# Orders by place, 64-row output products and TensorE's own waits in a fused attention and dense kernel

## The chip, the core and the metric

The kernel runs on one core of a Trainium2 chip. The metric is the device time of one execution in microseconds. A profiled execution comes with a trace of every instruction; TensorE does the matrix products (PE in the rows, PEld for its weight loads), VectorE is DVE, ScalarE is ACT, GpSimd is POOL, and SyncE is SP, which issues most DMAs.

## The reference

All inputs are float32; x is 2048 x 512, there are 32 heads of 16 columns, and the dense part is 1376 wide.

```python
xn = _layernorm(x)
qkv = (xn @ wqkv) -> q, k, v per head
p = softmax(q @ k.T * 16 ** -0.5)
s = (p @ v, heads side by side) @ wo
g = silu(gelu(xn @ w1 + b1) @ w2 + b2)
out = x + s * g
```

## The kernel before, in words

Products that must be exact are made of rounded halves: an operand is split into a high part (rounded) and a low part (the rest), and a product is three matmuls, high by high, high by low and low by high. The order of each engine's instructions is written out by hand: what stands earlier in the code stands earlier in that engine's queue.

**The dense part (first 476 us).** After the layer norm, the q, k and v projections and the two dense layers are made as pairs of 64-row matmuls: `run` walks two lists of operations, and `mm` (L590) issues one of them on the upper row tile (partitions 0 to 63, a = 0) and one on the lower (64 to 127, a = 1), so that two matmuls go side by side. An accumulator is written first by one row tile, later by the other. When `mm` changes the row tile of an accumulator whose last product isn't known to be over, it makes the matmul wait for a token: `mark` puts a copy of one element on ScalarE (`junk`, L604; twice on VectorE, L602) that waits for the latest product, and the matmul waits for that copy. `mark_early` does this from within the product before. Between the pairs, `fill` puts score tiles of the first units (below).

**The attention part.** The work is 32 units `u`: four heads by 512 queries. A unit has 16 steps of 128 keys, so step `n` has unit `n // 16` and place `n % 16`. A step's order is a string, `ORDER[3]` = T S X T T S T Y V:

- T (`t_one`, L739): scores of 128 keys by 512 queries of one head, on row tile 1, 1, 0, 0 in turn, with the rows' maxima subtracted by two extra rows; ScalarE makes their exponential (L741) into the tile that pv reads one step later. T's go to four PSUM banks.
- S (`s_whole`, L183, L189): scores the other way round, 128 queries by 512 keys, for a unit that comes later, only for the maximum that VectorE takes of them; the first S of a step is on row tile 0, the second on row tile 1.
- X and Y: one such tile of 512 columns in halves, X 256 columns on row tile 0, Y 256 columns on row tile 1 into the same bank. Y waits for X by a no-operation of TensorE that waits for TensorE's own semaphore. VectorE's maximum comes after Y.
- V (`pv_step`, L804): the exponentials of the step before times v, in four column tiles of 32, float32. After the last place of a unit VectorE copies the accumulator out (L811).

S, X and Y use three PSUM banks in turn (`s_ring`): an S takes the oldest bank and puts it at the end of the ring at once, an X takes the oldest bank and its Y puts it back. Score tiles run ahead of T, so from step 492 on there are none, and a step is T T T T V.

**The output product.** `at(n, f, ..., pos)` hangs a piece of work behind T number `pos` of step `n`. In steps 492 to 511 the first ten of sixteen token tiles of 128 rows are multiplied by `wo`. For tile `t`, with n = 492 + 2t: `load_gx` at n - 4 brings the dense result and x; `w_token` at n - 2 rounds the attention output (ScalarE L876, GpSimd L877); `w_mul` (`mm3`, L80) makes six 128-row matmuls at n and six at n + 1, into a bank of the ring; `gate` at n makes the gate (ScalarE L865, VectorE L866); `w_out` at n + 1 multiplies (VectorE L905), adds x (GpSimd L910) and stores. The other six tiles follow after the last step.

Of the kernel before, what the change touches and what calls it, by code (L numbers as in the profile page):

```python
# [8 lines left out]
F32 = mybir.dt.float32  # L9
F32R = mybir.dt.float32r  # L10
AF = mybir.ActivationFunctionType
# [5 lines left out]
P = 128  # L17
# [4 lines left out]
KT = D // P  # L22
NT = S // P
CH = 512
NCH = S // CH
# [10 lines left out]
DONE = 492  # L36
FILL0 = 30
HB = 4
W2B = 2
ORDER = {0: "TTTTV", 3: "TSXTTSTYV"}  # L40
HC = CH // 2
PAIRED = 28
KB = 3
# [5 lines left out]
def fused(ctx: ExitStack, tc: tile.TileContext, x, wqk, wv, wo, w1, b1, w2, b2, out):  # L49
    nc = tc.nc  # L50
# [17 lines left out]
    ident_r = keep.tile([P, P], F32R, name="ident_r")  # L68
# [17 lines left out]
    SYNC = mybir.DependencyInfo(mybir.DependencyClass.Sync, mybir.DependencyReason.DATA)  # L86
# [5 lines left out]
    def s_tile(held=False):  # L92
        pool = s_ring.pop(0)
        if not held:
            s_ring.append(pool)
        return pool.tile([P, CH], F32, name="ps"), pool
# [58 lines left out]
    done = {u: 0 for u in range(NU)}  # L155
# [30 lines left out]
    def s_max(ps, job, heads, parts):  # L186
        u, p = job[0], job[2]
        qi, ki = at_of(job)
        nc.vector.tensor_reduce(MX[u][:, 2 * p:2 * p + 2, qi, ki][:, heads, parts], ps.rearrange("p (n c) -> p n c", c=HC), axis=AX.X, op=OP.max)  # L189
        done[u] += 1  # L190
# [18 lines left out]
    def s_op(op):  # L209
# [6 lines left out]
        elif op == "X":  # L216
            if not cut:
                cut[:] = [jobs.pop(0), 0]
            ps, pool = s_tile(True)
            x = s_mm(ps, cut[0], 0, 0, cut[1] * HC, HC)  # L220
            cut[2:] = [ps, pool, x]
            run_off()
        else:
            job, n, ps, pool, x = cut
            hold = nc.tensor.nop().ins
            tc.add_manual_dep(hold, x.name, SYNC, reason="row tile done")
            s_mm(ps, job, 1, HC, n * HC, HC)
            s_max(ps, job, slice(0, 2), n)
# [33 lines left out]
    prog = {}  # L262
# [42 lines left out]
    for i in range(nu):  # L305
        pairs.append(ms[2 * i:2 * i + 2])
        if (i + 1) * len(qs) // nu > i * len(qs) // nu:
            g, c = qs[i * len(qs) // nu]
            pairs.append([("q", g, c), ("q", g, c + 1)])
    parts = [(c, f, h) for c in range(NCH) for f in range(FT) for h in range(2)]  # L310
    is_m = [pair[0][0] == "m" for pair in pairs]
    plan, nd = [("first", g, i) for g in range(VQ - 1) for i in (0, 2)], 0
    for j in range(len(pairs)):
        for h in range(2):
# [223 lines left out]
    keep_r = ctx.enter_context(tc.tile_pool(name="keep_r", bufs=1, side="right"))  # L538
# [19 lines left out]
    writer = {}  # L558
    s_when, put, row = [], [0], [0, 0]
# [22 lines left out]

    def mm(a, key, ps, lhs, rhs, first, last):
        r = slice(64 * a, 64 * a + 64)
        token = None
        if not first and writer[key][0] != a and writer[key][1] > prog["seen"]:
            if not tokens or tokens[-1][0] < writer[key][1]:
                mark()
            prog["seen"], token = next(x for x in tokens if x[0] >= writer[key][1])
        i = nc.tensor.matmul(ps, lhs[r], rhs[r], start=first, stop=last).ins  # L590
        if token is not None:
            tc.add_manual_dep(i, token, SYNC, reason="other row tile")
        prog["pe"] += 1
        row[a] += 1
        latest[0] = (prog["pe"], i.name)
        writer[key] = (a, prog["pe"])

    tokens, latest = [], [None]

    def mark(dve=False):  # L600
        if dve:
            i = nc.vector.tensor_copy(junk[:, 1:], ident_r[:1, :1].bitcast(F32)).ins  # L602
        else:
            i = nc.scalar.activation(junk[:, :1], ident_r[:1, :1].bitcast(F32), AF.Copy).ins  # L604
        tc.add_manual_dep(i, latest[0][1], SYNC, reason="row tile done")
        tokens.append((latest[0][0], i.name))

    def mark_early(n):
        if prog["seen"] < n:
            mark()  # L610

    junk = keep_r.tile([1, 2], F32, name="junk")

    def run(ops, hooks={}):
        for n, two in enumerate(zip(*ops)):
            prog["n"] += 1
            for a in range(2):
                fill(a)
                mm(a, *two[a])
            for h in hooks.get(n, []):  # L620
                h()
# [23 lines left out]
    def down(c, f, part):  # L645
        i = c * FT + f
        if f == 0 and part == 0:
            PA[c] = [ps_v.tile([P, D], F32, name="pv")] + [ps_t.tile([P, D], F32, name="pst") for t in range(3)]
        h, w = HS[c, f], W2[c, f]
        side = (part + i) % 2  # L650
        ops = [[], []]
        for a in range(2):
            for t in ((0, 1), (2, 3))[(a + side) % 2]:
                ts = slice(t * P, (t + 1) * P)
                for n, (x, y) in enumerate(((0, 0), (0, 1), (1, 0))):
                    ops[a].append(((c, t), PA[c][t], h[x][:, ts], w[y],
                                   f == 0 and part == 0 and n == 0, f == FT - 1 and part == 1 and n == 2))
        n = prog["pe"]
        if (c, f, part) == parts[-2]:
            run(ops, {2: [lambda: mark(True)], 5: [lambda: mark(True)]})  # L660
        else:
            run(ops, {3: [lambda: mark_early(n)]})
        if part == 0:
            w2_split(i + 1)
            w2_load(i + 3)
            return
        del HS[c, f], W2[c, f]
        if f == FT - 1:
            for t in (0, 2, 1, 3):
                gt = wk.tile([P, D], F32, name="gt", bufs=4)  # L670
                if c == NCH - 1:
                    nc.vector.tensor_add(gt, PA[c][t], b2_sb)  # L672
                else:
                    nc.scalar.activation(gt, PA[c][t], AF.Copy)
                rs = slice(c * CH + t * P, c * CH + (t + 1) * P)
                if c < NCH - 1:
                    chores.append((gt, rs))
                else:
                    nc.gpsimd.dma_start(g_d[rs, :], gt)
# [22 lines left out]
    def quad(n, at):  # L702
        us = first[n]
        for u, b in zip(us, BANKS[n]) if at == 0 else ():
            pool, name = {"x": (ps_x, "ps"), "m": (ps_m, "ps"), "v": (ps_v, "pv"), "t": (ps_t, "pst")}[b]
            PH[u] = pool.tile([P, CH], F32, name=name)
        for i in range(at, at + 2):
            hooks = {6: [mark]} if i in (1, 2) else {}
            if n == VQ - 2 and i in (0, 2):
                hooks[3] = [lambda: w1_split(0) if i == 0 else w1_load(1)]  # L710
            run((terms(us[i], 0, i < 2), terms(us[(i + 2) % 4], 1, i < 2)), hooks)
            if i >= 2:
                for u in (us[i - 2], us[i]):
                    v_out(u[1] * NCH + u[2], PH.pop(u))
# [62 lines left out]
    wb = ctx.enter_context(tc.tile_pool(name="work_b", bufs=2))  # L777
    ot = [slot(6 + c, (P, KT, CH)) if c < 2 else kp.tile([P, KT, CH], F32, name=f"ot{c}") for c in range(NCH)]
# [3 lines left out]
    wo_h = kp.tile([P, KT, D], F32R, name="wo_h")  # L782
    wo_l = kp.tile([P, KT, D], F32R, name="wo_l")
# [14 lines left out]
    def pv_step(u, k):  # L798
# [8 lines left out]
        if k == NT - 1:  # L807
# [36 lines left out]
    GX, OTS, PW, homes = {}, {}, {}, {}  # L844
# [47 lines left out]
    def w_mul(t, ks, parts=(0, 1)):  # L892
# [4 lines left out]
        for i, cs in enumerate(cols(t)):  # L897
            if i in parts:
                for k in ks:
                    mm3(PW[t][i][:, :cs.stop - cs.start], OTS[t, k], (wo_h[:, k, cs], wo_l[:, k, cs]),  # L900
                        k == 0, k == KT - 1)

    def w_gate(t, i=0):
        gx, cs = GX[t], cols(t)[i]
        nc.vector.scalar_tensor_tensor(gx[:, 0, cs], PW[t][i][:, :cs.stop - cs.start], 0.5, gx[:, 0, cs],  # L905
                                       op0=OP.mult, op1=OP.mult)
# [12 lines left out]
    def at(n, f, *a, pos=3):  # L919
        todo.setdefault((n, pos), []).append((f, a))  # L920

    KS = tuple(range(KT))
    L = 16 * NU

    def due(n):
        return min(4 * L, 4 * LEAD + max(0, 3 * n - 1))

    for u in range(NU):
        g, c = divmod(u, NCH)
# [15 lines left out]
    T3 = range(NT - NCH, NT)  # L945
    late = range(NW, NT)
    for t in range(NW):
        n = DONE + 2 * t
        at(n - 4, load_gx, t)
        at(n - 2, w_token, t)  # L950
        at(n, w_mul, t, KS[:2])
        at(n, gate, t)
        at(n + 1, w_mul, t, KS[2:])
        at(n + 1, w_out, t, nc.gpsimd)
    for i, t in enumerate(late):
        n = L - 2 * len(late) - 1 + 2 * i
        at(n - 4, load_gx, t)
# [8 lines left out]
    for n in range(L + 1):  # L966
        ua, ka = divmod(n, 16)
        want = due(n) - due(n - 1)
        i = 0
        for op in ORDER[want] if n > 1 else ("TTTTV", "TTSTSVT")[n]:  # L970
            if op in "SXY":
                s_op(op)
            elif op == "V":
                if n:
                    pv_step(*divmod(n - 1, 16))
                for _ in range(4):
                    tick()
# [61 lines left out]
```

## Time and profile before

| | |
|---|---|
| median of three runs | 1581.37 us (1580.71 to 1581.43) |
| the profiled execution | 1580.84 us |
| its span in the trace | 1579.0 us |
| TensorE, weight loads | 1572.2, 949.2 us busy |
| VectorE, ScalarE, GpSimd | 1396.2, 1247.6, 373.6 us busy |
| granted TensorE clock | full (1.0) throughout |

A row of a timeline has the start in the span, the time that it took, the engine, the line, the operation, what it writes and reads, rows*columns and the shape, and a count where several follow one another; in brackets stands the idle time before it and what ended it. A row of the waits has who waited for whom, the sum in us, the number of times and the longest. Starts are what the argument goes by, since matmuls overlap and their ends are modelled. PSUM tiles `ps` and `pst` are score banks, `pv` is the accumulator of V.

### The profile page before, as it was taken

How to read it: one execution, taken by the hardware profiler on the slowest of the kernel's cores; microseconds unless marked ns; L12 is line 12 of the kernel's file. 1: busy time of each engine (PE TensorE's matmuls, PEld its weight loads, DVE VectorE, ACT ScalarE, POOL GpSimd, SP SyncE). 2: the span in 40 equal slices, each digit the busy share in tenths (PEclk: the TensorE clock that was granted, in tenths of full speed). 3: DMA queues.
4: the chain of work that ended last, by engine and by line, in shares of the span. 5: the costliest groups of instructions: out<-in, count | busy, mean ns of one | idle time of the engine just before them, and what ended most of it. 6: DMA issues, size and time to landing. Idle time of an engine off the chain costs nothing.

```text
span 1579.0 us, 31736 instructions
## 1 busy us (share of the span) xinstructions
PE 1572.2 (100%) x12144; PEld 949.2 (60%) x12144; DVE 1396.2 (88%) x2292; ACT 1247.6 (79%) x2489; POOL 373.6 (24%) x394
## 2 busy tenths in 40 slices
PE   9999999999999999999999999999999999999998
PEld 8899899999994444444444444444444444444445
DVE  7599898989988999999999999999999999999734
ACT  4333443434339999999999999999999999999984
POOL 4145575766641001001000100100100000000143
PEclk9999999999999999999999999999999999999999
DMA  6626343454322114111511511421150111110252
GB/s 207 151 59 154 116 138 99 147 150 122 123 84 76 43 33 68 29 36 42 82 30 29 69 38 34 56 45 29 30 76 24 33 29 36 36 30 22 60 194 101
DMA packets 74647, 116.86 MB, mean 74 GB/s; under 512 B 23012, under 2 KB 24292, under 8 KB 73320
## 3 DMA queue, kind: packets, MB, share of 16 engines
q1 hardware_dynamic: 70748, 101.89, 24.1%
q0 software_dynamic: 3264, 12.35, 4.7%
q8 instruction: 96, 1.57, 0.5%
q10 hardware_dynamic: 484, 0.60, 0.1%
q14 instruction: 55, 0.45, 0.1%
HBM read 84.35 MB, written 25.97 MB: 70 GB/s over the span
## 4 chain that ended last, share of the span: by engine, by line
PE 98%; DVE 1%; DMA 0%; issue 0%; ACT 0%; DVEq 0%
PE pv L804 33%; PE pst L739 21%; PE ps L590 13%; PE ps L183 10%; PE pst L590 7%; PE ps L739 7%; PE ps L80 3%; PE pv L590 2%; PE ps L458 1%; PE pst L80 1%; DVE st L417 0%; PE pst L440 0%; DMA xt<-in_x 0%; PE pst L458 0%; DVE slot L75 0%; DVE xn L431 0%
## 5 line engine op out<-in xcount | busy, mean ns | idle before, releaser
L189 DVE TENSOR_REDUCE mx<-ps 128x2 f32<-128x512 f32 x2048 | 1298.3, 685 | 118.6 <-PE ps L183 33.0
L741 ACT ACTIVATE slot<-pst 128x512 f32<-128x512 f32 x1533 | 825.9, 603 | 19.9 <-PE pst L739 10.5
L804 PE MATMUL pv<-slot,vsb 128*32 128x512 f32 x4096 | 545.3, 605 | 0.0
L183 PE MATMUL ps<-kt,slot 48*128 48x512 f32 x1364 | 376.4, 366 | 0.0
L739 PE MATMUL pst<-qt,kt 50*128 50x512 f32 x1149 | 372.3, 431 | 0.6 <-DVE gt L672 0.4
L739 PEld LDWEIGHTS pst<-qt,kt 50*128 50x128 f32 x1149 | 188.6, 184 | 288.3 <-ACT slot L741 261.8
L741 ACT ACTIVATE slot<-ps 128x512 f32<-128x512 f32 x515 | 311.2, 605 | 2.7 <-PE ps L183 1.8
L183 PEld LDWEIGHTS ps<-kt,slot 48*128 48x128 f32 x1364 | 224.7, 184 | 8.2 <-DVE mx L189 5.9
L590 PE MATMUL ps<-slot,w1h 64*128 64x512 f32 x1088 | 218.0, 393 | 0.0
L183 PE MATMUL ps<-kt,qz 48*128 48x512 f32 x512 | 212.8, 416 | 0.0
L183 PE MATMUL ps<-slot,slot 48*128 48x512 f32 x598 | 165.5, 366 | 0.0
L739 PE MATMUL ps<-qt,kt 50*128 50x512 f32 x387 | 159.7, 415 | 0.0
L590 PEld LDWEIGHTS ps<-slot,w1h 64*128 64x128 f32 x1088 | 151.2, 185 | 8.2 <-ACT junk L604 2.4
L590 PE MATMUL ps<-slot,w1l 64*128 64x512 f32 x544 | 141.8, 393 | 0.0
L804 PEld LDWEIGHTS pv<-slot,vsb 128*32 128x32 f32 x4096 | 80.6, 108 | 100.0 <-issue 91.8
L377 POOL TENSOR_TENSOR hl<-hg,hh 128x512 fp32r<-128x512 f32 x76 | 96.7, 1295 | 129.6 <-ACT hh L376 97.5
L250 POOL CAST nmh<-nm 128x16 fp32r<-128x16 f32 x32 | 6.3, 196 | 480.4 <-DVE nm L247 458.0
L604 ACT ACTIVATE junk<-ident_r 1x1 f32<-1x1 f32 x92 | 18.0, 196 | 119.3 <-PE pst L590 116.1
L739 PE MATMUL pst<-qt,slot 50*128 50x512 f32 x384 | 111.2, 414 | 0.0
L183 PEld LDWEIGHTS ps<-kt,qz 48*128 48x128 f32 x512 | 93.7, 183 | 15.6
L183 PEld LDWEIGHTS ps<-slot,slot 48*128 48x128 f32 x598 | 98.3, 184 | 3.1 <-DVE mx L189 2.1
L739 PEld LDWEIGHTS ps<-qt,kt 50*128 50x128 f32 x387 | 71.1, 184 | 42.1 <-ACT slot L741 36.4
(159 smaller groups left out, 1707.2 us busy)
## 6 DMA issues: line engine op xcount, KB each, us to landing
raw<-in_w SPq DMA_DIRECT2D x88, 256.0 KB
qk_h<-hh SPq DMA_DIRECT2D x32, 256.0 KB
qk_l<-hl SPq DMA_DIRECT2D x32, 256.0 KB
qt<-qk_h SPq DMA_DIRECT2D x128, 64.0 KB
slot<-qk_h SPq DMA_DIRECT2D x92, 64.0 KB
g_d<-gt POOLq DMA_DIRECT2D x16, 256.0 KB, 3.8
qt<-qk_l SPq DMA_DIRECT2D x64, 64.0 KB
dn<-den_d SPq DMA_DIRECT2D x32, 128.0 KB
```

The source lines that it names most:

```text
L80: nc.tensor.matmul(ps, lhs[a], rhs[b], start=first and n == 0, stop=last and n == 2)
L183: return nc.tensor.matmul(ps[:, c0:c0 + w], QS[u][r, p, qi * P:(qi + 1) * P], kts[u // NCH % KB][p][r, k0:k0 + w], start=True, stop=True).ins
L189: nc.vector.tensor_reduce(MX[u][:, 2 * p:2 * p + 2, qi, ki][:, heads, parts], ps.rearrange("p (n c) -> p n c", c=HC), axis=AX.X, op=OP.max)
L250: nc.gpsimd.tensor_copy(hl[:, 0], nm)
L377: nc.gpsimd.tensor_sub(hl, raw, hh.bitcast(F32))
L458: nc.tensor.matmul(pq["q", g, c], W1[g][i][:, k * P:(k + 1) * P], (xh, xl)[j][c][:, k], start=n == 0 and k == 0, stop=n == 2 and k == KT - 1)
L590: i = nc.tensor.matmul(ps, lhs[r], rhs[r], start=first, stop=last).ins
L604: i = nc.scalar.activation(junk[:, :1], ident_r[:1, :1].bitcast(F32), AF.Copy).ins
L739: nc.tensor.matmul(ps, kts[g % KB][p][r, k * P:(k + 1) * P], QT[u][r, p, :], start=True, stop=True)
L741: nc.scalar.activation(PT[u, k][:, 2 * p + a, :], ps, AF.Exp, scale=SCALE)
L804: nc.tensor.matmul(PV[u][32 * j:32 * j + 32, :], vsb[:, k, h:h + 32], PT[u, k][:, j, :], start=(k == 0), stop=(k == NT - 1))
```

## The change

Three things, each in its place.

1. Where a step has score tiles and isn't in unit 0, its order goes by its place in the unit: place 0 has S T X T T S T Y V, place 2 has X T S T T Y S T V. The other places keep the order of before.
2. The ten token tiles go in pairs, four steps to a pair. `w_two` rounds two key blocks (of four) of both tiles in one pass. `w_halves` issues six 64-row matmuls, one on each row tile in turn: on side 0 row tile 0 adds to the first tile and row tile 1 to the second, on side 1 the other way round. Two such blocks stand in each step, behind the second and the fourth T. Every block that follows a change of side or of key blocks begins with a no-operation that waits for the last product of the block before. Loads, gates and stores move with it: both tiles of a pair are stored at the pair's fourth step.
3. In `mm`, the matmul that changes the row tile waits, by a no-operation of TensorE, for the accumulator's last product itself. `mark`, `mark_early`, their tokens and the tile `junk` are gone.

```diff
 ORDER = {0: "TTTTV", 3: "TSXTTSTYV"}
+AFTER = {0: "STXTTSTYV", 2: "XTSTTYSTV"}
...
         if not first and writer[key][0] != a and writer[key][1] > prog["seen"]:
-            if not tokens or tokens[-1][0] < writer[key][1]:
-                mark()
-            prog["seen"], token = next(x for x in tokens if x[0] >= writer[key][1])
+            hold = nc.tensor.nop().ins
+            tc.add_manual_dep(hold, writer[key][2], SYNC, reason="other row tile")
+            prog["seen"] = writer[key][1]
         i = nc.tensor.matmul(ps, lhs[r], rhs[r], start=first, stop=last).ins
-        if token is not None:
-            tc.add_manual_dep(i, token, SYNC, reason="other row tile")
...
-            run(ops, {3: [lambda: mark_early(n)]})
+        run(ops)
...
+    def w_two(t, k0):
+        oh, ol = [wb.tile([P, KT, P], F32R, name=x, bufs=3) for x in ("oh", "ol")]
+        c, i = divmod(t, NCH)
+        src = ot[c][:, k0:k0 + 2, i * P:(i + 2) * P]
+        hi, lo = [w.rearrange("p (k t) s -> p k (t s)", t=2) for w in (oh, ol)]
+        nc.scalar.activation(hi, src, AF.Copy)
+        nc.gpsimd.tensor_sub(lo, src, hi.bitcast(F32))
...
+    def w_halves(t, k, side):
+        ts = (t, t + 1)
+        if k == 0 and side == 0:
+            for i in ts:
+                PW[i] = [s_tile()[0]]
+        elif k % 2 == 0:
+            hold = nc.tensor.nop().ins
+            tc.add_manual_dep(hold, HALF[0].name, SYNC, reason="row tile done")
+        for n, (x, y) in enumerate(((0, 0), (0, 1), (1, 0))):
+            for a in range(2):
+                i = ts[a ^ side]
+                r = slice(64 * a, 64 * a + 64)
+                HALF[0] = nc.tensor.matmul(PW[i][0], OTS[i, k][x][r], (wo_h, wo_l)[y][r, k],
+                                           start=k == 0 and side == 0 and n == 0,
+                                           stop=k == KT - 1 and side == 1 and n == 2).ins
...
     for t in range(NW):
-        n = DONE + 2 * t
-        at(n - 4, load_gx, t)
-        at(n - 2, w_token, t)
-        at(n, w_mul, t, KS[:2])
-        at(n, gate, t)
-        at(n + 1, w_mul, t, KS[2:])
-        at(n + 1, w_out, t, nc.gpsimd)
+        n = DONE + 4 * (t // 2)
+        at(n - 3 + t % 2, load_gx, t)
+        if t % 2 == 0:
+            for i in range(4):
+                if i % 2 == 0:
+                    at(n + i - 2, w_two, t, i)
+                for j in range(2):
+                    at(n + i, w_halves, t, i // 2 * 2 + j, i % 2, pos=1 + 2 * j)
+        at(n + t % 2, gate, t)
+        at(n + 3, w_out, t, nc.gpsimd)
...
-        for op in ORDER[want] if n > 1 else ("TTTTV", "TTSTSVT")[n]:
+        order = ORDER[want] if n > 1 else ("TTTTV", "TTSTSVT")[n]
+        if want == 3 and ua:
+            order = AFTER.get(ka, order)
+        for op in order:
```

More of the change, by code (lines that the diff above doesn't have):

```diff
@@ L584, in mm @@
         r = slice(64 * a, 64 * a + 64)
-        token = None
         if not first and writer[key][0] != a and writer[key][1] > prog["seen"]:
-            if not tokens or tokens[-1][0] < writer[key][1]:
-                mark()
-            prog["seen"], token = next(x for x in tokens if x[0] >= writer[key][1])
+            hold = nc.tensor.nop().ins
+            tc.add_manual_dep(hold, writer[key][2], SYNC, reason="other row tile")
+            prog["seen"] = writer[key][1]
         i = nc.tensor.matmul(ps, lhs[r], rhs[r], start=first, stop=last).ins
-        if token is not None:
-            tc.add_manual_dep(i, token, SYNC, reason="other row tile")
         prog["pe"] += 1
         row[a] += 1
[L595 to L612, printed above, removed]
+        writer[key] = (a, prog["pe"], i.name)
     def run(ops, hooks={}):
@@ L657, in down @@
                                    f == 0 and part == 0 and n == 0, f == FT - 1 and part == 1 and n == 2))
[L658 to L661, printed above, removed]
-            run(ops, {3: [lambda: mark_early(n)]})
+        run(ops)
         if part == 0:
@@ L707, in quad @@
         for i in range(at, at + 2):
-            hooks = {6: [mark]} if i in (1, 2) else {}
+            hooks = {}
             if n == VQ - 2 and i in (0, 2):
@@ L901, in w_mul @@
                         k == 0, k == KT - 1)
+    def w_two(t, k0):
[5 more added lines that the diff above has]
+        nc.gpsimd.tensor_sub(lo, src, hi.bitcast(F32))
+        for k in range(2):
+            for j in range(2):
+                OTS[t + j, k0 + k] = (oh[:, 2 * k + j], ol[:, 2 * k + j])
+    HALF = {}
+    def w_halves(t, k, side):
[13 more added lines that the diff above has]
+                                           stop=k == KT - 1 and side == 1 and n == 2).ins
     def w_gate(t, i=0):
@@ L947, in fused @@
     for t in range(NW):
-        n = DONE + 2 * t
-        at(n - 4, load_gx, t)
-        at(n - 2, w_token, t)
-        at(n, w_mul, t, KS[:2])
-        at(n, gate, t)
-        at(n + 1, w_mul, t, KS[2:])
-        at(n + 1, w_out, t, nc.gpsimd)
+        n = DONE + 4 * (t // 2)
[4 more added lines that the diff above has]
+                    at(n + i - 2, w_two, t, i)
+                for j in range(2):
+                    at(n + i, w_halves, t, i // 2 * 2 + j, i % 2, pos=1 + 2 * j)
+        at(n + t % 2, gate, t)
+        at(n + 3, w_out, t, nc.gpsimd)
     for i, t in enumerate(late):
```

## The prediction

> **What bounds the kernel now.** I read the page first (busy shares, then the chain that ended last), then the waits, then the timeline of TensorE, VectorE and ScalarE around the places that the diff touches. All numbers are of the profiled execution: 1580.84 us, of which the span is 1579.0; the median of the three timed runs, 1581.37, is 0.53 above it.
>
> ```profile
> PE 1572.2 (100%) x12144; PEld 949.2 (60%) x12144; DVE 1396.2 (88%) x2292; ACT 1247.6 (79%) x2489; POOL 373.6 (24%) x394
> PE 98%; DVE 1%; DMA 0%; issue 0%; ACT 0%; DVEq 0%
> PEld ps L183 <- DVE mx L189: 8.1, 30, 0.3
> PEld ps L590 <- ACT junk L604: 2.4, 9, 0.3
> ```
>
> TensorE holds 98% of the chain, so a microsecond taken off its stream is a microsecond off the span, and work of the other engines counts only where TensorE waits for it. A busy TensorE is not a full one, though, and the last two rows say where it stands still in the two places that the diff names: 30 waits of a score tile for a VectorE maximum, 0.3 us each, and 9 waits in the dense part for a ScalarE marker. Thirty is also the number of units (1 to 30) to which the new orders apply.
>
> **Edit 1, the orders at places 0 and 2 of a unit.** This is place 1 and place 2 of unit 5 (steps 81 and 82). TensorE comes first, its weight loads next, VectorE last.
>
> ```profile
> 642.26 0.49 PE L739 MATMUL pst<-qt,kt 50*128 50x512 f32 x1
> 642.95 0.39 PE L739 MATMUL pst<-qt,kt 50*128 50x512 f32 x1
> 643.07 0.28 PE L183 MATMUL ps<-kt,slot 48*128 48x256 f32 x1
> 643.31 1.06 PE L804 MATMUL pv<-slot,vsb 128*32 128x512 f32 x8
> 644.31 0.50 PE L739 MATMUL pst<-qt,kt 50*128 50x512 f32 x1
> 644.31 0.61 PE L183 MATMUL ps<-kt,slot 48*128 48x512 f32 x2
> 644.65 0.39 PE L739 MATMUL pst<-qt,kt 50*128 50x512 f32 x1
> 644.76 0.39 PE L739 MATMUL ps<-qt,kt 50*128 50x512 f32 x1
> 645.11 0.49 PE L183 MATMUL ps<-kt,slot 48*128 48x512 f32 x1
> 645.11 0.50 PE L739 MATMUL pst<-qt,kt 50*128 50x512 f32 x1
> 645.45 0.28 PE L183 MATMUL ps<-kt,slot 48*128 48x256 f32 x1
> 645.65 1.06 PE L804 MATMUL pv<-slot,vsb 128*32 128x512 f32 x8
> 645.11 0.18 PEld L183 LDWEIGHTS ps<-kt,slot 48*128 48x128 f32 x1 [0.27 <-DVE mx L189]
> 642.58 0.68 DVE L811 COPY os<-pv 128x512 f32<-128x512 f32 x1
> 643.17 3.76 DVE L189 TENSOR_REDUCE mx<-ps 128x2 f32<-128x512 f32 x6
> 647.21 0.69 DVE L189 TENSOR_REDUCE mx<-ps 128x2 f32<-128x512 f32 x1 [0.28 <-PE ps L183]
> ```
>
> Step 81 takes 643.31 - 642.26 = 1.05 us from its first matmul to its pv product. Step 82 takes 645.65 - 644.31 = 1.34: 0.29 more. The reason stands below it: VectorE evacuates the old unit's output (the copy at 642.58) ahead of the three maxima of step 81, and from 643.17 on it runs six maxima without a pause, 0.6 us apart. The second whole score tile (S) of step 82 writes the third bank of the ring, the one that the third of these maxima (the split tile Y of step 81) reads last. It starts at 645.11, and a wait at the head of TensorE's queue also holds back the T and the Y behind it.
>
> The new order of place 2, X T S T T Y S T, does not bring that maximum forward. The bank is still the third of the ring, because X, S and S take the three banks in turn in either order, so the second S still loads at 645.11. What changes is what is left behind it: before, a T beside it on the other row tile and then a Y of 256 columns; now only the T beside it, since Y has gone ahead. Y started at 645.45, the two before it end at 645.60 and 645.61, so pv can start after these. The pv of step 82 started 0.08 before the modelled end of the Y (645.45 + 0.28 = 645.73); by the same 0.08 before 645.61 it starts at 645.53 to 645.54. That is 0.11 us a unit, 30 x 0.11 = 3.3 us. From above it is bounded by the whole 0.29 (8.7 us), if the maxima came sooner; from below by a loss of about 0.1 a unit (3 us), since X in the first slot fills only half of it, and the first maximum of step 82 can start later when its tile is second. I take 3.2, nearest to the two matmul ends. The next step has room: its first S needs a bank that VectorE has by then read, and the seventh maximum (647.21) waited for TensorE again, so the backlog ends there.
>
> At place 0 the first S changes places with the first T. The two run on different row tiles and start together (644.31 and 644.31 in the step shown), so this moves a maximum by hundredths at most: 0.
>
> **Edit 2, the ten token tiles in 64-row pairs.** Steps 492 to 511 have no score tiles left; each has four T, half a token's product (six matmuls, L80) and pv.
>
> ```profile
> 1520.42 1.06 PE L804 MATMUL pv<-slot,vsb 128*32 128x512 f32 x8
> 1521.42 0.73 PE L739 MATMUL pst<-qt,kt 50*128 50x512 f32 x3
> 1521.77 0.39 PE L739 MATMUL ps<-qt,kt 50*128 50x512 f32 x1
> 1522.08 0.50 PE L80 MATMUL ps<-wo_h,oh 128*128 128x512 f32 x1
> 1523.34 0.40 PE L80 MATMUL ps<-wo_h,ol 128*128 128x512 f32 x1
> 1523.67 1.06 PE L804 MATMUL pv<-slot,vsb 128*32 128x512 f32 x8
> 160.70 0.61 PE L590 MATMUL pst<-w2h,hh 64*128 64x512 f32 x2
> 160.93 0.61 PE L590 MATMUL pst<-w2l,hh 64*128 64x512 f32 x2
> 161.16 0.61 PE L590 MATMUL pst<-w2h,hl 64*128 64x512 f32 x2
> 161.67 0.50 PE L590 MATMUL ps<-slot,w1h 64*128 64x512 f32 x1
> 1520.62 0.65 ACT L865 ACTIVATE slot<-gx 128x512 f32<-128x512 f32 x1
> 1521.14 0.65 ACT L876 ACTIVATE oh<-slot 128x512 fp32r<-128x512 f32 x1
> ```
>
> A step is 1523.67 - 1520.42 = 3.25 us: pv to T 1.00, T to the first L80 0.66, L80 to pv 1.59. The change does the same arithmetic in twelve 64-row matmuls a step, two side by side. The dense part runs this very shape (64*128, 512 columns), and its rows show two matmuls per 0.23 us (160.70, 160.93, 161.16), so six pairs cost what six 128-row matmuls cost, about 1.40. What goes is a change of array form: T, L80 and pv are three forms now, two after. To price this I take step 81 above: its row tiles carry 3.5 slots of 512 columns each in 1.05 us; at 0.234 a slot that leaves 0.23 for filling and for the change to pv. A new step has eight slots on each row tile (two T and six products): 0.23 + 8 x 0.234 = 2.10 against 0.66 + 1.59 = 2.25. It saves 0.15 a step, 20 x 0.15 = 3.0 us. With slots of 0.226 it would be 4.2, with 0.24 some 2.0.
>
> The sum needs the two row tiles to go on independently, since T and T follow each other on one row tile, then three pairs, then T and T on the other. The four T of the step above answer this: two pairs that each share a row tile take 0.66 us with filling, which is two slots, so the later pair passed the earlier one. If matmuls could start only in the order of issue, these four would need three slots, and a new step nine. The Trainium skill (TensorE: Matmul & The Clock Gate, Part 3, packing small matmuls) states exactly that rule: matmuls start and end in program order, and only weight loads are pulled ahead. By that rule a step would be 2.34 instead of 2.10 and this edit would lose 1.8 us; the trace disagrees with it at this place (0.66 us).
>
> Step 492 is longer than the others, and there the new place of the blocks helps too.
>
> ```profile
> 1490.19 1.06 PE L804 MATMUL pv<-slot,vsb 128*32 128x512 f32 x8
> 1494.26 0.64 PE L804 MATMUL pv<-slot,vsb 128*32 128x512 f32 x4
> 1491.73 0.18 PEld L739 LDWEIGHTS pst<-qt,kt 50*128 50x128 f32 x1 [0.26 <-ACT slot L741]
> 1492.22 0.18 PEld L739 LDWEIGHTS ps<-qt,kt 50*128 50x128 f32 x1 [0.31 <-ACT slot L741]
> ```
>
> It takes 4.07, 0.82 over 3.25, because the third and fourth T wait for ScalarE, which is behind after the score steps. With three pairs of products now between the second and third T (0.70 us), most of that 0.57 is covered: 0.5 (0 to 0.8). Edit 2 is 3.0 + 0.5 = 3.5 us.
>
> Its covers: ScalarE's work in four steps is sixteen exponentials and six other passes, 0.48 to 0.52 each by the starts above (1520.62, 1521.14), 10.8 us or 2.7 a step; new steps of 3.10 hide that, and ScalarE becomes the bound if TensorE's step falls below it. The rounding of a pair's tiles is asked two steps before use as before; VectorE reads a pair's two banks one after the other, which can hold the second pair of tokens back once, by up to 0.25. The hold ahead of a block waits for a product of the step before, with a whole pv between: nothing. At the end two token outputs instead of one stand in POOL's and SP's queues:
>
> ```profile
> 1557.01 1.28 POOL L910 TENSOR_TENSOR gx<-gx 128x512 f32<-128x512 f32 x1 [1.33 <-DVE gx L905]
> 1558.99 1.16 SPq L827 DMA_DIRECT2D ot<-os  x2
> 1561.41 0.33 SPq L833 DMA_DIRECT2D den_d<-dr  x1
> ```
>
> The second addition (1.28) delays SP's two moves to about 1560.0, done by 1561.15, and the store of the denominators at 1561.41 still finds SP free: 0 (up to 0.5 if it doesn't).
>
> **Edit 3, the dense waits.** Twelve matmuls wait for a product of the other row tile. So far each waits for a marker that ScalarE (twice VectorE) sets when a later product has ended; now for that product itself, ten times fourteen or more matmuls back.
>
> ```profile
> L604 ACT ACTIVATE junk<-ident_r 1x1 f32<-1x1 f32 x92 | 18.0, 196 | 119.3 <-PE pst L590 116.1
> ```
>
> The marker comes late: 161.67 above stands 0.51 after 161.16, where 0.23 is usual. The loads were idle 2.4 us in nine such waits; the loads run ahead of the products, so I count half, 1.2 us (0 to 2.4). A product fourteen matmuls back started 1.6 us earlier and took 0.61 at most, so the new wait is over before it is asked; only the last two holds, six matmuls back, can cost about 0.1 each. The 92 markers leave 18.0 us of ScalarE; TensorE waits for ScalarE nowhere else there, so this is worth nothing. The hold is a wait at the head of TensorE's queue, and what is queued behind it is the next products of both row tiles.
>
> **Sum.** 3.2 + 3.5 + 1.2 = 7.9 us: the profiled execution would go from 1580.84 to 1572.9, the median from 1581.37 to 1573.5.
>
> **Rivals.** (a) Edit 1 gives nothing, since the second S waits for the same maximum and a T still ends the step: 1576.7. For it: the wait itself is untouched. Against it: Y's 0.11 goes. (b) Edit 1 takes the whole 0.29: 5.5 us more, 1568.0; it needs maxima that end sooner, and VectorE has no pause to give. (c) Matmuls start in the order of issue, nine slots in a new step: 20 x 0.234 = 4.7 us worse, 1578.2; the 0.66 speaks against it. (d) A wait for TensorE's own semaphore empties the array: 12 dense and 15 late holds at the 0.3 of the last waits' row, 8.1 us, so that about 1581.6 comes out, no change; but every Y waits that way already, and the Y at 643.07 follows its T at 642.95 by 0.12, without a gap. (e) Slower: the two row tiles do not run side by side in the new blocks, because the halves of the same two tokens alternate between two banks. A step then has six slots more, 6 x 0.234 x 20 = 28 us, 1601.6. It decides once a block of three pairs takes over 0.9 us instead of 0.70, for then the other gains are eaten. The dense pairs, which share banks in the same manner over time, speak against it.
>
> **How the numbers follow.** Three timed runs agree within 0.72 us, so 0.2%, 3.2 us, is about what a measurement can tell from no change. Forecast 0.57 (its own range 1570 to 1576), (a) 0.19, (b) 0.07, (c) 0.05, (d) 0.05, (e) 0.04, other 0.03, mostly no change or slower. Faster (below 1578.2): 0.57 + 0.19 + 0.07 + half of (c) = 0.86; same: half of (c), (d) = 0.08; slower: (e) and other = 0.06. The range reaches from (b), 1568, to 1579, which takes in (a), (c) and the small ends of all three terms.
>
> **What would show it.** Right: steps of place 2 at 2.23 us instead of 2.34 from pv to pv, with the S wait still there; late steps of 3.10; the first late step near 3.4; no gap of 0.5 at the dense holds. Wrong: place 2 near 2.04 or above 2.34, late steps above 3.25, or new idle time of TensorE behind a hold.

## The result, and the profile after

The changed kernel takes 1573.42 us (median, 1573.18 to 1573.82) against 1581.18 for the kernel before on the same chip (1580.71 to 1581.51): ratio 0.9951, 95% interval 0.9941 to 0.9962. The predicted time was 1573.5. The profiled execution took 1573.31 us, its span is 1571.4.

A step's time below is the distance from its predecessor's first pv row to its own. The mean of a place is over units 1 to 30. The table compares the two profiled spans by stage, in us.

| stage | before | after | change | predicted |
|---|---|---|---|---|
| start to first pv | 477.77 | 476.86 | -0.91 | -1.2 |
| first pv to step 491 | 1012.42 | 1009.07 | -3.34 | -3.2 |
| steps 492 to 511 | 65.94 | 62.11 | -3.84 | -3.5 |
| last pv step to the end | 22.88 | 23.40 | +0.53 | 0 |

The page of the kernel after: the busy shares, the chain by engine, and from the waits the row of score tiles waiting for VectorE.

```profile
PE 1564.2 (100%) x12264; PEld 952.0 (61%) x12264; DVE 1397.1 (89%) x2290; ACT 1233.8 (79%) x2397; POOL 371.9 (24%) x394
PE 98%; DVE 1%; ACT 0%; DMA 0%; issue 0%; DVEq 0%
PEld ps L184 <- DVE mx L190: 50.5, 61, 0.8
```

TensorE still holds 98% of the chain and is busy for 8.0 us less (1572.2 before), about the gain. The waits row misleads: 50.5 us replace 8.1, though the kernel is faster. In the rows of both kernels the loads pause for 0.84 us ahead of a step's first load, while pv runs. With X or S first in a step, this pause is put down to the maximum that had freed its bank earlier (first row below); at 60 places, two in each of thirty units, that would make 50.4. In the dense part the row of loads that waited for ScalarE's marker (2.4 us before) is gone.

The timeline of the weight load, TensorE and VectorE in place 2 of unit 5 (the step shown in the prediction), with the kernel after:

```profile
642.96 0.18 PEld L184 LDWEIGHTS ps<-kt,slot 48*128 48x128 f32 x1 [0.84 <-DVE mx L190]
642.96 0.38 PE L184 MATMUL ps<-kt,slot 48*128 48x256 f32 x1
642.96 0.50 PE L716 MATMUL pst<-qt,kt 50*128 50x512 f32 x1
643.18 0.43 PE L184 MATMUL ps<-kt,slot 48*128 48x512 f32 x1
643.30 0.40 PE L716 MATMUL pst<-qt,kt 50*128 50x512 f32 x1
643.45 0.40 PE L716 MATMUL ps<-qt,kt 50*128 50x512 f32 x1
643.54 0.67 PE L184 MATMUL ps<-kt,slot 48*128 48x256 f32 x2
643.72 0.49 PE L716 MATMUL pst<-qt,kt 50*128 50x512 f32 x1
644.14 1.07 PE L781 MATMUL pv<-slot,vsb 128*32 128x512 f32 x8
641.78 3.75 DVE L190 TENSOR_REDUCE mx<-ps 128x2 f32<-128x512 f32 x6
```

From the first matmul to pv it takes 644.14 - 642.96 = 1.18 us (before 1.34, predicted 1.23). Y starts at 643.54, the second S and the last T end the step, and VectorE still runs six maxima without a pause. A late step, 64-row pairs on both row tiles:

```profile
1508.20 1.07 PE L781 MATMUL pv<-slot,vsb 128*32 128x512 f32 x8
1509.20 0.49 PE L716 MATMUL pst<-qt,kt 50*128 50x512 f32 x1
1509.54 0.38 PE L905 MATMUL ps<-wo_l,oh 64*128 64x512 f32 x1
1510.92 0.41 PE L905 MATMUL ps<-wo_h,ol 64*128 64x512 f32 x2
1511.26 1.06 PE L781 MATMUL pv<-slot,vsb 128*32 128x512 f32 x8
```

It takes 3.06 us, and T to pv 2.06. A slot, the distance from one 512-column matmul to the next on the same row tile, is (1510.92 - 1509.54) / 6 = 0.23; eight of them leave 0.22 for the rest.

### The profile page after: what moved, and what is told of

The parts are those of the page before. It is cut to its first block, busy times and chain, and to the rows that moved or that the text cites. A ratio compares the mean times of both kernels' runs of the same rounds, so it can differ in the third digit from the quotient of the medians.

```text
span 1571.4 us, 31849 instructions
## 1 busy us (share of the span) xinstructions
PE 1564.2 (100%) x12264; PEld 952.0 (61%) x12264; DVE 1397.1 (89%) x2290; ACT 1233.8 (79%) x2397; POOL 371.9 (24%) x394
## 4 chain that ended last, share of the span: by engine, by line
PE 98%; DVE 1%; ACT 0%; DMA 0%; issue 0%; DVEq 0%
PE pv L781 33%; PE pst L716 20%; PE ps L590 13%; PE ps L184 12%; PE pst L590 7%; PE ps L716 6%; PE pv L590 2%; PE ps L905 1%; PE ps L81 1%; PE ps L459 1%; PE pst L81 1%; DVE st L418 0%; PE pst L441 0%; DMA xt<-in_x 0%; PE pst L459 0%
## 5 line engine op out<-in xcount | busy, mean ns | idle before, releaser
L716 PE MATMUL pst<-qt,kt 50*128 50x512 f32 x1149 | 380.3, 430 | 0.6 <-DVE gt L649 0.4
L184 PE MATMUL ps<-kt,slot 48*128 48x512 f32 (+1 forms) x1364 | 377.4, 367 | 0.0
L184 PE MATMUL ps<-slot,slot 48*128 48x512 f32 (+1 forms) x598 | 165.7, 366 | 0.0
L590 PEld LDWEIGHTS ps<-slot,w1h 64*128 64x128 f32 x1088 | 154.4, 185 | 4.6
L371 ACT ACTIVATE hg<-ps,b_sb 128x512 f32<-128x512 f32 x44 | 27.8, 684 | 132.7 <-PE ps L590 116.9
```

Of the source, the lines that this page charges most:

```text
L184: return nc.tensor.matmul(ps[:, c0:c0 + w], QS[u][r, p, qi * P:(qi + 1) * P], kts[u // NCH % KB][p][r, k0:k0 + w], start=True, stop=True).ins
L371: nc.scalar.activation(raw, ph.pop(u), AF.Gelu_apprx_tanh, bias=b1_sb[:, u[2]:u[2] + 1])
L716: nc.tensor.matmul(ps, kts[g % KB][p][r, k * P:(k + 1) * P], QT[u][r, p, :], start=True, stop=True)
```

## The experiments

**The parts, each alone.** Theory: the terms of the sum are independent, and place 0 is worth nothing. Four kernels were timed on one chip, where the kernel before took 1580.33 us.

```diff
 place2:  +AFTER = {2: "XTSTTYSTV"}     (edit 1 without place 0)
 place0:  +AFTER = {0: "STXTTSTYV"}     (edit 1 without place 2)
 halves:  w_two, w_halves and their places (edit 2)
 holds:   mm waits by a TensorE no-operation; mark, mark_early gone (edit 3)
```

> The kernel before with the new order at place 2 alone, X T S T T Y S T. Theory (Y goes ahead of the S that waits for VectorE): 0.14 us in each of the 23 units whose place 3 has no extra work on VectorE, nothing in the seven units divisible by 4, in all -3.2 us, so 1578.0 (ratio 0.998), with place 2 near 2.19 and place 3 near 2.05 us. Rival (place 0 carries part of it, or the two orders need each other): less than -2 us here, 1579.3 or more.

> The kernel before with the new order at place 0 alone, S T X T T S T Y. Theory (the first S and T start together in either order): no change, 0 +- 0.3 us, 1581.2. Rival (the S's maximum starts earlier and shortens VectorE's backlog): place 0 goes from 2.046 to 2.036 and place 2 gets shorter as well, -0.5 to -1 us or more, 1580.5.

> The kernel before with the ten token tiles in 64-row pairs alone. Theory (array form changes go, row tiles run independently): steps 492 to 511 shorter by 3.8 us, the part after the last step longer by 0.5: -3.3 us, 1577.9 (ratio 0.998), with settled steps of 3.07 us. Rival (a part of the gain came from the other two edits, or the later stores eat it): -2 us or less.

> The kernel before with the dense waits by TensorE's own semaphore alone. Theory: the dense part is shorter by 0.9 us (six visible load gaps of 0.2 to 0.3 us less what the holds cost), nothing else moves: 1580.3 (ratio 0.9994). Rival (the later part gives it back, since ScalarE and VectorE start the attention part in other positions): 0 +- 0.3 us, 1581.2.

| kernel | median us | saved | ratio (95%) | in its stage of the profiled span |
|---|---|---|---|---|
| place 2 alone | 1577.91 | 2.42 | 0.9984 (0.9975 to 0.9993) | 1012.42 to 1009.78: -2.64 |
| place 0 alone | 1579.15 | 1.18 | 0.9993 (0.9985 to 1.0002) | 1012.42 to 1011.27: -1.15 |
| pairs alone | 1576.67 | 3.66 | 0.9977 (0.9968 to 0.9987) | 65.94 to 62.11: -3.83; end +0.33 |
| dense waits alone | 1579.67 | 0.66 | 0.9996 (0.9987 to 1.0005) | see early_mark below |

The four savings add to 7.92 us, the whole saved 7.76. Two of the intervals hold 1, so for these the trace decides. How far a trace can be trusted here shows in kernels that share a stage: the four traced kernels with the orders of before and the whole copy (before, pairs alone, dense waits alone, and the early marker below) take 1012.15 to 1012.46 us from the first pv to step 491, and the three with both new orders at places 0 and 2 (after, and by row and late below) 1008.98 to 1009.24. The 1011.27 of place 0 alone is clear of both.

The surprise is place 0, where the rival came true and not the theory: the mean of place 2 goes from 2.339 to 2.297 with place 0 alone, and by the same 0.04 once more, from 2.225 to 2.187, where place 2 is changed as well. Four rows of each kernel show how: the first matmul of place 0 (step 80), the first maximum of that step, and the second S of place 2 (step 82) two steps later. Before, then place 0 alone:

```profile
640.21 0.49 PE L739 MATMUL pst<-qt,kt 50*128 50x512 f32 x1
640.21 0.50 PE L183 MATMUL ps<-kt,slot 48*128 48x512 f32 x1
640.77 0.69 DVE L189 TENSOR_REDUCE mx<-ps 128x2 f32<-128x512 f32 x1
645.11 0.49 PE L183 MATMUL ps<-kt,slot 48*128 48x512 f32 x1
```

```profile
639.49 0.49 PE L184 MATMUL ps<-kt,slot 48*128 48x512 f32 x1
639.50 0.50 PE L740 MATMUL pst<-qt,kt 50*128 50x512 f32 x1
640.02 0.69 DVE L190 TENSOR_REDUCE mx<-ps 128x2 f32<-128x512 f32 x1
644.36 0.49 PE L184 MATMUL ps<-kt,slot 48*128 48x512 f32 x1
```

From the first maximum to the waiting S it is 4.34 us in both: VectorE runs through three maxima, the copy and three more without a pause. The first maximum stands 0.56 behind the step's first matmul before and 0.53 now, and these 0.03 arrive undiminished two steps later. Over the thirty units the first distance falls from a mean of 0.568 to 0.534, and the second stays between 4.33 and 4.34 in both kernels.

**Is the wait the copy's?** VectorE copies 16 columns of a unit's output instead of 512, so this kernel leaves out most of the attention output.

```diff
-                nc.vector.tensor_copy(OS[u], pv)
+                w = CH if u == 0 else DH          # OS[u]: one tile kept for all units
+                nc.vector.tensor_copy(OS[u][:, :w], pv[:, :w])
```

> The kernel before, but VectorE copies only 16 of the 512 columns of each unit's output from unit 1 on (most of the attention output is left out). Theory (the wait at place 2 is the copy's 0.6 us that VectorE hasn't caught up by then, and the first maximum at place 0 counts only because VectorE runs without a pause from there on): place 2 falls from 2.339 to about 2.04 us in every unit, place 3 of every unit stays at 2.01, in all -9 us, a span near 1569.5. Rival (the wait is set by the banks or by TensorE's own order, whatever stands in VectorE's queue): place 2 stays above 2.25.

This kernel, the order T S X T T Y S T at place 2, the run by row and the early marker below were timed once each (1572.69, 1577.70, 1573.44 and 1580.06 us, the kernel before 1581.32 beside them); for these the argument goes by the traces.

The span was 1570.8 against 1579.5 for the kernel before on the same chip; place 2 fell to a mean of 2.042 (2.01 to 2.07 but for unit 1, where the whole output of unit 0 is copied, at 2.34), and the stage from the first pv to step 491 by 8.1 us. VectorE's timeline at the same places shows that it pauses for TensorE again (0.16 us ahead of the fourth maximum):

```profile
641.75 0.17 DVE L815 COPY os<-pv 128x16 f32<-128x16 f32 x1
641.97 1.89 DVE L189 TENSOR_REDUCE mx<-ps 128x2 f32<-128x512 f32 x3
644.02 2.71 DVE L189 TENSOR_REDUCE mx<-ps 128x2 f32<-128x512 f32 x4 [0.16 <-PE pst L739]
```

So the wait at place 2 comes from the copy, behind which the next maximum started 0.6 us later (642.58 and 643.17 before) and starts 0.22 us later here. One part of the expectation failed: place 3 did not stay at 2.01 everywhere. In the seven units divisible by 4 (4, 8 to 28) it is 2.20 to 2.23, and in the kernel after it is 2.18 to 2.19 there. Place 3 of unit 4 in the kernel after, VectorE and then TensorE:

```profile
611.13 0.28 DVE L248 TENSOR_REDUCE nm<-mx 128x16 f32<-128x128 f32 x1
611.32 3.16 DVE L190 TENSOR_REDUCE mx<-ps 128x2 f32<-128x512 f32 x5
612.47 0.40 PE L716 MATMUL pst<-qt,kt 50*128 50x512 f32 x1
612.65 0.50 PE L184 MATMUL ps<-kt,slot 48*128 48x512 f32 x1
```

In these units the scores of a later unit end at place 2, and VectorE makes their common maximum (L248, 0.28 us) in the middle of its backlog. As long as place 2 waited 0.3 us this was hidden behind that wait; now the second S of place 3 pays, 0.17 a time.

**What in the order of place 2 counts?** Y ahead of S, but S ahead of X as before.

```diff
+AFTER = {2: "TSXTTYSTV"}
```

> The kernel before with T S X T T Y S T at place 2: Y goes ahead of the second S as in the change, but the first S keeps its place ahead of X. Theory (what counts is only what is queued behind the S that waits): place 2 at 2.22 to 2.23, as with X first (2.225). Rivals: X in front is needed to keep the row tiles filled (2.27 or more); or X in front costs, as it puts the first maximum back (2.20 or less).

Place 2 took 2.226 us, as the theory had it. The next two runs show that this agreement was a coincidence.

**The same order where the wait came back, and everywhere.**

```diff
 orders:      -AFTER = {0: "STXTTSTYV", 2: "XTSTTYSTV"}
              +AFTER = {0: "STXTTSTYV", 2: "TSXTTYSTV"}
              +            if ka == 3 and ua % 4 == 0 or ka == 4 and ua % 8 == 4:
              +                order = AFTER[2]
 everywhere:  +AFTER = {k: "STXTTYSTV" for k in range(16)}     (on top of "both", below)
```

> The kernel after the change, with T S X T T Y S T instead of X T S T T Y S T at place 2, and that same order also at place 3 of the units divisible by 4 and at place 4 of every second of these (4, 12, 20, 28), where the wait for VectorE came back. Theory (only what is queued behind the waiting S counts, in whatever step it waits, and X in front puts the first maximum of place 2 back): place 2 stays at 2.19, place 3 of the seven units goes from 2.18 to about 2.08 and place 4 of the four from 2.21 to about 2.10 us; from the first pv to step 491 about 1.2 to 1.6 us less than 1009.07, a time near 1572.0. Rival (the wait at place 3 is only what place 2 no longer waits for, and goes on to place 4 or 5 when it is taken away again): 1009.0 +- 0.3, 1573.4.

> As the kernel with both, but every step with score tiles after unit 0 has S T X T T Y S T. Theory (Y ahead of S helps only where S waits for VectorE; elsewhere the step ends with a 512-column tile instead of a 256-column one): the other places get 0.02 to 0.05 us longer, +10 to +20 us in all. Rival (the order costs nothing where nothing waits, and the orders need not go by place): within 1 us of the kernel with both.

Both theories fell, and the rivals beside them too. The kernel with these orders took 1574.84 us, 0.9962 of before (0.9948 to 0.9975). Against the kernel after, whose stage is 1009.07, it needs 1010.91: place 2 went up from 2.187 to 2.217, place 3 of the seven units from 2.18 to 2.22, and place 4 of the four from 2.21 to 2.41. With the order in every step it was 1651.62 us, ratio 1.0448 (1.0433 to 1.0462), and the means of all places were 2.22 to 2.25 us, waiting for VectorE or not. The timeline of TensorE in place 2 of unit 5 with these orders gives the reason:

```profile
643.89 0.51 PE L716 MATMUL pst<-qt,kt 50*128 50x512 f32 x1
643.89 0.61 PE L184 MATMUL ps<-kt,slot 48*128 48x512 f32 x2
644.24 0.39 PE L716 MATMUL pst<-qt,kt 50*128 50x512 f32 x1
644.34 0.40 PE L716 MATMUL ps<-qt,kt 50*128 50x512 f32 x1
644.56 0.38 PE L184 MATMUL ps<-kt,slot 48*128 48x256 f32 x1
644.65 0.50 PE L716 MATMUL pst<-qt,kt 50*128 50x512 f32 x1
644.78 0.39 PE L184 MATMUL ps<-kt,slot 48*128 48x512 f32 x1
645.10 1.07 PE L781 MATMUL pv<-slot,vsb 128*32 128x512 f32 x8
```

Y waits at the head of TensorE's queue until X is over. X is the second of the x2, which are over at 643.89 + 0.61 = 644.50, and Y starts at 644.56. Behind it a T and a whole S are still to come, so pv starts 1.21 after the first matmul, with or without a wait for VectorE. What the hold costs shows beside step 81 of the kernel before, which has the same work and no wait; these rows stand between the T's that the prediction shows:

```profile
642.60 0.28 PE L183 MATMUL ps<-kt,slot 48*128 48x256 f32 x1
642.72 0.39 PE L739 MATMUL ps<-qt,kt 50*128 50x512 f32 x1
642.83 0.40 PE L183 MATMUL ps<-kt,slot 48*128 48x512 f32 x1
```

There the S that follows the second T on row tile 1 starts 642.83 - 642.26 = 0.57 behind the first matmul; the held Y, in the same position, starts at 0.67. Behind a half, the next matmul on its row tile came after 0.12 (642.60 and 642.72); behind the held Y it comes after 0.22. The last T, on the other row tile, stands at 0.76 instead of 0.69. Together they put pv back from 1.05 to 1.21. The order of the tiles differs as well, with a whole S last instead of a half, and no run takes out the hold alone, so the share of the hold rests on these rows.

In the kernel after, X is first (642.96) and over by 643.34, and Y follows at 643.54 with nothing lost. So X in front is not decoration, as I had taken it: it takes the hold of Y off the path. Place 4 had been misread as well: its 0.2 is no wait for VectorE but one transpose (L268) that takes TensorE from 614.20 to 614.40 ahead of the T's (the kernel after, unit 4).

```profile
614.20 0.27 PE L268 MATMUL pst<-ident_r,nmh 128*64 128x128 f32 x1
614.40 0.49 PE L716 MATMUL pst<-qt,kt 50*128 50x512 f32 x1
```

**Do the row tiles depend on the order of issue?** Each block of six issues row tile 0's three products first.

```diff
-        for n, (x, y) in enumerate(((0, 0), (0, 1), (1, 0))):
-            for a in range(2):
+        for a in range(2):
+            for n, (x, y) in enumerate(((0, 0), (0, 1), (1, 0))):
```

> The kernel after the change, but each block of six 64-row products issues the three of row tile 0 first, then the three of row tile 1. Theory (each row tile works through its own matmuls, whatever the order of issue between them): late steps stay at 3.06 to 3.10 us, span 1571.4 +- 0.7. Rival (matmuls start in the order of issue): two slots of 0.234 more in each of two blocks, up to 0.94 a step, so steps up to 4.0 and some 9 to 19 us more.

Settled steps took 3.065 us, as in the kernel after (3.064), and the span 1571.6 against 1571.4. The timeline of one step:

```profile
1510.13 0.39 PE L905 MATMUL ps<-wo_l,oh 64*128 64x512 f32 x1
1510.35 0.40 PE L905 MATMUL ps<-wo_h,oh 64*128 64x512 f32 x1
1510.36 0.39 PE L905 MATMUL ps<-wo_h,ol 64*128 64x512 f32 x1
1510.59 0.39 PE L905 MATMUL ps<-wo_l,oh 64*128 64x512 f32 x1
1510.60 0.40 PE L716 MATMUL pst<-qt,kt 50*128 50x512 f32 x1
1510.82 0.39 PE L905 MATMUL ps<-wo_h,ol 64*128 64x512 f32 x1
1510.83 0.39 PE L716 MATMUL ps<-qt,kt 50*128 50x512 f32 x1
```

The T of 1510.60 is the step's third, on row tile 0. The code issues it after all six products, yet it starts 0.22 us before the last of them (1510.82, row tile 1). The Trainium skill (TensorE: Matmul & The Clock Gate, Part 3, packing small matmuls) says that matmuls start in program order; between two row tiles this trace shows otherwise.

**Why were the dense waits late?** ScalarE still sets the marker, but is asked at the first pair of the next part.

```diff
-            run(ops, {3: [lambda: mark_early(n)]})
+            run(ops, {0: [lambda: mark_early(n)]})
```

> The kernel before, but in the dense part the marker ScalarE sets for a product of the part before is asked at the first pair of the next part instead of the fourth; the engine that sets it stays the same. Theory (the waits were the marker's lateness, 116.1 of 119.3 us of its idle time being waits for TensorE): from the first dense product to the first pv 425.7 becomes about 425.0, as with TensorE's own waits (424.76 and 425.22). Rival (the crossing to another engine and back costs, however early): 425.7 +- 0.2, no change.

From the first dense product to the first pv it took 425.04 us. The six kernels with the old markers, this one apart, took 425.56 to 426.26 (mean 425.84); the seven with TensorE's own waits 424.76 to 425.25 (mean 425.07), all below them. Of the waits of the dense products for the marker, this row is what is left (2.4 before):

```profile
PEld ps L590 <- ACT junk L604: 0.4, 1, 0.4
```

So the cost was that the marker was asked late; which engine sets it matters little. Edit 3 is worth 0.8 us. The -0.91 of the table holds 0.22 more, by which the first dense product came earlier (51.64 against 51.86); this start varies from 51.45 to 52.42 over all kernels, so it is no part of the gain.

**A version that repairs the new waits.** In the kernel after, steps 496 and 497 take 3.28 and 3.40 us instead of 3.06. The loads and VectorE there:

```profile
1499.92 0.18 PEld L905 LDWEIGHTS ps<-wo_h,oh 64*128 64x128 f32 x1 [0.17 <-DVE gx L911]
1503.11 1.37 DVE L843 SCALAR_TENSOR_TENSOR gx<-slot,gx 128x512 f32<-128x512 f32 x1 [3.25 <-ACT slot L842]
1504.41 0.68 DVE L788 COPY os<-pv 128x512 f32<-128x512 f32 x1
```

The second pair's bank waits for VectorE's second multiplication; and the unit's copy, without which the next unit's pv can't start, stands behind a gate that waits for ScalarE. The two waits cover each other: in the run by row step 496 has no wait (3.08), yet step 497 takes 3.60, and both together take 6.68 there as in the kernel after. So the gate sets the sum of the two steps, and the bank's wait alone was worth nothing.

```diff
 late:  +            if t == 2:
        +                s_ring.insert(0, s_ring.pop())
        -        at(n + t % 2, gate, t)
        +        at(n + (t % 2 or t == 2), gate, t)
        the stores of tokens 8 and 9 issued after o_den(NU - 1)
 both:  late and orders together
```

> The kernel after the change, with three edits behind the score steps: the second pair of tokens takes the bank that was free longest, its first gate is made a step later, and the stores of the last pair go behind the moves and the denominators of the last unit. Theory: step 496 falls from 3.28 to 3.07 and step 497 from 3.40 to 3.07 (the second bank had waited for VectorE's second multiplication, and the unit's copy stood behind a gate that waited for ScalarE), and the part after the last step from 23.40 to 22.9, as the small denominator move no longer shares the DMA engines with a store: 1.0 us in all, 1572.4. Rivals: the waits go to the steps beside them (496 to 499 keep 0.3 or more above 3.07), or the part after the last step varies by itself (22.9 to 23.4 whatever the order of the stores).

> The two kernels above in one. If their savings are independent: the sum of the two, 2.2 to 2.6 us below the kernel after the change, about 1571 us.

With the late edits alone: 1572.45 us (1572.26 to 1572.6), ratio 0.9946 (0.9934 to 0.9959) to 1581.01 before. Steps 496 and 497 both take 3.07, the twenty late steps 61.59 instead of 62.11, and the steps beside them are as they were. The edits of the bank and of the gate were made together, so neither is measured alone. VectorE's copy now waits for pv alone:

```profile
1502.69 0.69 DVE L788 COPY os<-pv 128x512 f32<-128x512 f32 x1 [2.80 <-PE pv L781]
```

It is the fastest version here. Its interval overlaps that of the kernel after, and they were compared with the kernel before on different occasions, so that it is ahead (8.6 us saved against 7.8) rests on the 0.52 us of the trace. With the orders of above on top it was 1574.29 us, ratio 0.9958 (0.9945 to 0.9970): late steps of 61.59 and a stage of 1010.92, the two effects side by side. The sum of about 1571 that was expected fell with the orders. The third edit, the stores, stays open: the part after the last step took 22.95 us in two kernels with it and 23.15 in a third, without it 23.40, 23.41, 23.20, but also 22.95 (the kernel that issues by row), so the order of the stores alone doesn't set it.

## Why the prediction was right, and where only by luck

The forecast of 1573.5 lies 0.08 from the measured median, and that closeness is luck: by the table the three parts and the end were off by +0.14, +0.34, -0.29 and -0.53 us of gain, which largely cancel. The three mechanisms are what held. Edits 1 and 2 came near their sizes, edit 1 by two errors of 1.2 us that cancel; edit 3 came to two thirds of its. In the chances, (e) and other add to 0.07 rather than the 0.06 given; nothing hangs on it.

**Edit 1: 3.2 predicted, 3.34 measured, with three errors in it.** The 0.11 at place 2 was right for its order (2.339 to 2.225 alone). (1) "So this moves a maximum by hundredths at most: 0" was the mis-sized term: the hundredths are 0.04 at place 2, 1.2 us over thirty units, since VectorE has no pause in between. The prediction had even shown half of that unbroken run of VectorE. (2) "The backlog ends there" was wrong in seven units, where VectorE's reduction for a later unit prolongs it: +0.17 x 7 = 1.2 us the other way. By places, thirty times the changes of the means, steps up to 491 alone: place 2 -4.56, place 3 +1.26, place 1 +0.45, place 4 -0.54, place 0 -0.30, the rest +0.33, in all -3.4. (3) "What changes is what is left behind it" was only half the reason: with Y ahead but X not in front, the step has a floor of 2.22 by the hold of Y, which the prediction didn't price. Its rival of a gain of the whole 0.29 failed, but what it needed, maxima that come sooner, came in part: 0.04 of the 0.29.

**Edit 2: 3.5 predicted, 3.84 measured.** The two row tiles go on independently, as the four T had shown, and a step has eight slots. Settled steps fell to 3.06, not 3.10, because a slot is 0.23 rather than 0.234 and the rest 0.22 rather than 0.23: 0.18 a step instead of 0.15. That this piece is the change of array form rests on the sum of slots; no run changes the form alone. Step 492 fell by 0.90 (predicted 0.65), 493 by 0.20. "Can hold the second pair back once, by up to 0.25" was right for step 496 in size (0.22), but the run by row shows that this wait was covered by the next. Step 497 (0.33) was not foreseen: moving the gate put VectorE's copy behind a wait for ScalarE, a queue that the prediction didn't go through for this.

**Edit 3: 1.2 predicted, 0.8 measured.** The visible waits went as predicted; counting half of 2.4 us was too much, a third would have been right.

**The end: 0 predicted, +0.53 in this profile**, the upper end given for it; over the four kernels with pairs and the stores in this order it is 22.95 to 23.41, against 22.87 to 22.96 in the seven kernels without pairs: a cost between nothing and 0.5 that varies from trace to trace, with no cause shown.

**The rivals.** The start in order of issue and the row tiles that don't run side by side are refuted by the settled steps of 3.06 and the run by row. The rival that a wait for TensorE's own semaphore costs 0.3 each time is refuted too: the dense part with these waits got shorter by 0.8, and the late steps with their holds take the 3.06 that slots and filling make up. Such a wait stopped TensorE's queue where its product was still running, as at Y above.

## What to carry to other kernels

Where an engine runs without a pause up to the wait that counts, its first instruction's start is worth its whole value there, hundredths included: follow the run back to its last pause and reorder at that place. A no-operation that waits at the head of a queue was free here where its producer was already over (edit 3), and cost where it was not (Y); move the producer to the front before moving the consumer. And when a wait is shortened, list what else had been hidden behind it (here a reduction every fourth unit), and walk every queue that a moved step passes. A wait that shows in a timeline is not yet a price: the next one may cover it, as at steps 496 and 497.

## What the runs showed of the hardware that I had not expected

The two row tiles started their matmuls like two queues of their own: a matmul on row tile 0 started 0.22 us before one of row tile 1 that had been issued ahead of it, and the order of issue within a block of six made no difference to a step (3.065 and 3.064 us). A no-operation that waits in TensorE's queue held back the T on the other row tile too (0.76 instead of 0.69). With the order that has such a hold close behind its other half in every step, the mean of places 3 to 11 rose from 2.04 to 2.23 us.
